# One over rms by exp and ln on ScalarE in place of a power on GpSimd, and a fourth buffer of float64 words

## Chip, cores and metric

One core of a Trainium2 chip runs the whole kernel. The metric is the device time of one execution in microseconds (us). Several executions agree within some 0.3%.

## The reference, cut to what matters

Attention with normalised queries and keys, and behind it two stages of dense layers, all in float32:

```python
q_n = q / sqrt(mean(q * q) + 1e-6) * g_q          # k_n alike with g_k; over the 64 of a head
scores = q_n @ k_n.T / 8
attn = exp(scores - max) / (sum + 1e-9)
x = attn @ v                                       # 4 batches, 12 heads, 448 rows, 64 columns
h = x @ w_in;  x = maximum(0.01 * h, h) @ w_out    # 768 -> 2048 -> 768, 1792 rows
y = ((x @ w1) * (x @ w2)) @ w3 @ w_last            # 768 -> 1024 -> 1024 -> 768
```

The weights come as float64. Each product is made of three matmuls: every operand is split into a high and a low part (`wh`, `wl`; `xh`, `xl`), and high x high, high x low and low x high are added up.

## The kernel before, in words

TensorE (PE) does all products and transposes, ScalarE (ACT) exp, copies and the rounding to the high parts, VectorE (DVE) the low parts, sums and reductions, GpSimd (POOL) the normalisation of the softmax and some subtractions. SyncE's queue (SP) issues most loads; ACT's queue issues loads of weights, POOL's the stores of converted weights.

**Attention** goes by pairs of heads, 24 of them, t from 0 to 23. `load_rows` (L127) loads the rows of q and k of a pair three pairs ahead. `statistics` (L137), also three pairs ahead, squares them on ACT (L149), sums on DVE (L150), makes mean plus epsilon `ss` (L151) and takes it to the power of -0.5 on POOL (L153), with a tile `power` full of -0.5; L154 scales the part of q. `keys` (L192) multiplies the rows of k (L200), transposes them on PE into `pk` (L205), and writes the high and low keys `kh` on ACT (L214) and `kl` on DVE (L215), two buffers each. The transposes are told to come behind the last scores of the pair before. `scores` (L221) makes the scores, DVE moves them from PSUM into tiles `p` (L250), nine buffers, ACT applies exp in place (L259), DVE makes the reciprocal of the sums (L264, L265), POOL normalises (L268). `p_transpose` (L275) transposes p on PE (L282), DVE and ACT copy the result (L104, L102). `values` multiplies with v.

**Weights.** The class `Weights` converts float64 words to float32 by integer arithmetic: a load of a tile's words (`load`, L386; the DMA is L398) into `w64`, three buffers; `to_float32` (L400) with one instruction on POOL (L416), two on ACT (L418, L421) and two on DVE (L423, L427); `split` (L430) with the rounding on ACT (L452) and the low part on DVE (L180), and where a tile is needed again stores of it from POOL's queue (L444, L455). The first three loads are issued by SP's queue once the queries of the second pair are on their way; each later one by ACT's queue, behind the rounding of the tile that was split last (`self.rounded`). `work` (L459) sets the order: split tile t, load tile t+3, convert tile t+1.

**Order.** The attention's steps and the dense layers' matmuls are interleaved by `fill`, which spends an estimated time of matmuls per step; the conversions are pulled by the matmuls (`pump`) two tiles ahead. A scheduler with a timing model then sets each engine's order from these steps, their priorities and `issue_after`. The first pairs come alone; the product of the two last weight matrices begins with the fifth pair. Batches 0 and 1 go through the dense layers beside the attention, two groups of weights for batch 0 alone; these are stored and loaded again for batch 1. From some 820 us only the last two batches' dense layers are left.

Of the kernel before, what the change touches and what calls it, by code (L numbers as in the profile page):

```python
# [8 lines left out]
F32 = mybir.dt.float32  # L9
F32R = mybir.dt.float32r  # L10
U32 = mybir.dt.uint32
AF = mybir.ActivationFunctionType
ALU = mybir.AluOpType
# [4 lines left out]
B, H, S, D = 4, 12, 448, 64  # L18
NT = B * S
DM, FF, F2 = 768, 2048, 1024  # L20
P = 128
CP = 112
NCH = S // CP
# [11 lines left out]
CONVERT_PRIORITY = 100  # L35
STATS_AHEAD = 3
KEYS_AHEAD = 1
P_TILES = 9
TOGETHER = 2000
COMBINE_SLOTS = 5, 17  # L40
EARLY = 2
# [6 lines left out]
def attention_then_moe(  # L48
# [22 lines left out]
    nc = tc.nc  # L71
# [4 lines left out]
    def right(**kw):  # L76
        return heads_only.enter_context(tc.tile_pool(side="right", **kw))

    const = ctx.enter_context(tc.tile_pool(name="const", bufs=1))
# [2 lines left out]
    io = right(name="io", bufs=2)  # L82
    att = right(name="att", bufs=2)
    small = right(name="small", bufs=4)
    cv = right(name="cv", bufs=3)
    dram = ctx.enter_context(tc.tile_pool(name="dram", bufs=1, space=DRAM))
    psum = ctx.enter_context(tc.tile_pool(name="psum", bufs=8, space=PSUM))

    def bank(name):
        return psum.tile([P, 512], F32, tag="ps", name=name)  # L90
# [2 lines left out]
    ident = const.tile([P, P], F32, name="ident")  # L93
    gg = const.tile([P, 2], F32, name="gg")
    gqk = const.tile([P, 1], F32, name="gqk")
    power = const.tile([CP, 2, 2, NCH], F32, name="power")
    wc = dram.tile([NO, P, K2, P], F32, name="wc")
    xd = dram.tile([B - PB, KD, P, S], F32, name="xd")

# [12 lines left out]
    start = {}  # L112
# [14 lines left out]
    def load_rows(t):  # L127

        if t >= NH // 2:
            return  # L130
        b, j = divmod(2 * t, H)
        x = pairs[t]["rows"] = io.tile([CP, 2, 2, NCH, D], F32, tag="qk", name="qk_sb", bufs=2)
        for part in (1, 0):
            src = qk[b, j : j + 2, :, part].rearrange("h p c d -> p h c d")
            start["dma"] = nc.sync.dma_start(x[:, part], src)

    def statistics(t):  # L137

        if t >= NH // 2:
            return  # L140
        x = pairs[t]["rows"]
        ss = small.tile([CP, 2, 2, NCH], F32, tag="ss", name="ss", bufs=2)
        after = exps.get(t - STATS_AHEAD)
        for part in (1, 0):
            y = x[:, part]
            if part:
                y = io.tile([CP, 2, NCH, D], F32, tag="sq", name="sq", bufs=1)
            with tc.issue_after(after.ins) if after else ExitStack():
                nc.scalar.activation(y, x[:, part], AF.Square)  # L149
            nc.vector.tensor_reduce(ss[:, part], y, axis=AX.X, op=ALU.add)  # L150
        nc.vector.tensor_scalar(ss, ss, 1.0 / D, 1e-6, op0=ALU.mult, op1=ALU.add)  # L151
        rs = small.tile([CP, 2, 2, NCH], F32, tag="rs", name="rs", bufs=4)
        nc.gpsimd.tensor_tensor(rs, ss, power, op=ALU.pow)  # L153
        nc.vector.tensor_scalar_mul(rs[:, 0], rs[:, 0], -1.0 / D**0.5)  # L154
        pairs[t]["scale"], pairs[t]["rk"] = rs[:, 0], rs[:, 1]

    def load(t):

        if t >= NH // 2:
            return  # L160
        b, j = divmod(2 * t, H)
        pairs[t]["qt"] = io.tile([P, S], F32, tag="qt", name="qt_sb")
        dma = nc.sync.dma_start(pairs[t]["qt"], qt[b, j : j + 2].rearrange("h d s -> (h d) s"))
        start["dma"] = dma
        if t == 1:
            start["ins"] = dma
# [15 lines left out]
    def prep(t):  # L182

        if t >= NH // 2:
            return
        x = pairs[t]
        x["qh"] = att.tile([P, S], F32R, tag="qh", name="qh", bufs=2)
        copy("A", x["qh"], x["qt"])
        x["ql"] = att.tile([P, S], F32R, tag="ql", name="ql", bufs=2)
        subtract("P", x["ql"], x["qt"], x["qh"])  # L190

    def keys(t):  # L192

        if t >= NH // 2:
            return
        x = pairs[t].pop("rows")
        kn = x[:, 0].rearrange("p h c d -> p (h c d)")
        kn = kn.rearrange("p (c h d) -> p c h d", c=NCH, h=2)
        rk = pairs[t]["rk"].unsqueeze(3).to_broadcast([CP, 2, NCH, D])
        nc.vector.tensor_tensor(kn.rearrange("p c h d -> p h c d"), x[:, 1], rk, op=ALU.mult)  # L200
        pk = bank("pk")
        scored = pairs[t - 1].get("scored") if t else None
        with tc.issue_after(scored.ins) if scored else ExitStack():
            for c in range(NCH):
                nc.tensor.transpose(  # L205
                    pk[:, c * CP : (c + 1) * CP],
                    kn[:, c].rearrange("p h d -> p (h d)"),
                    ident[:CP, :CP],
                )
        x = [att.tile([P, S], F32R, tag=part, name=part, bufs=2) for part in ("kh", "kl")]  # L210
        pairs[t]["kh"], pairs[t]["kl"] = x
        kh, kl = (y.rearrange("q (p c) -> q p c", c=NCH) for y in x)
        pk = pk[:, :S].rearrange("q (c p) -> q p c", c=NCH)
        one = nc.scalar.activation(kh, pk, AF.Copy, scale=gqk)  # L214
        nc.vector.scalar_tensor_tensor(  # L215
            kl, pk, gqk, kh.bitcast(F32), op0=ALU.mult, op1=ALU.subtract
        )
        if t == 0:
            start["keys"] = one

    def scores(t, half):  # L221
# [24 lines left out]
        for c in chunks:  # L246
            for e, h in enumerate(pair):
                p = h["p"][c] = att.tile([CP, S], F32, tag="p", name="p", bufs=P_TILES)
                low = small.tile([CP, 1], F32, tag="low", name="low", bufs=8)
# [88 lines left out]
    def attention_steps():  # L338

        for t in range(NH // 2 + 2):  # L340
            ranked(values, t - 2)
            yield 2 * t
            for half in range(2):
                s = 2 * t + half
                for kc in range(NCH):
                    ranked(p_transpose, s - 2, kc)
                    yield s
                ranked(scores, t, half)
                for _ in range(NCH):
                    yield s  # L350
                if half:
                    ranked(keys, t + KEYS_AHEAD)
                    ranked(load, t + 2)
                    ranked(statistics, t + STATS_AHEAD)
                else:
                    load_v(2 * t)
                    ranked(prep, t + 1)
                    load_rows(t + STATS_AHEAD)
                run_later()
                yield s  # L360


    class Weights:
# [22 lines left out]
        def load(self, t):  # L386
            src, wide = self.sources[t][:2]
            n = self.size(t)
            if isinstance(src, tuple):
                return  # L390
            if not wide:
                self.raw[t] = wp.tile([P, WT], F32, tag="raw", name="raw")
                nc.sync.dma_start(self.raw[t][:, :n], src)
                return
            x = self.words[t] = cv.tile([P, WT, 2], U32, tag="w64", name="w64")
            eng = nc.sync if t < 3 else nc.scalar
            with tc.issue_after((start["ins"] if t < 3 else self.rounded).ins):
                eng.dma_start(x[:, :n], src.rearrange("p (n t) -> p n t", t=2))  # L398

        def to_float32(self, t):  # L400
# [57 lines left out]

        def work(self):  # L459
            n = len(self.sources)  # L460
            for t in range(-3, n):
                if t >= 0:
                    self.split(t)
                    yield
                for u, wide in ((t + 2, False), (t + 3, True)):
                    if 0 <= u < n and self.sources[u][1] == wide:
                        self.load(u)
                        yield
                if 0 <= t + 1 < n and self.sources[t + 1][1]:
                    yield from self.to_float32(t + 1)  # L470
# [479 lines left out]


    with tc.high_priority():
        nc.vector.memset(power, -0.5)
        make_identity(nc, ident)
        load_rows(0)
        statistics(0)
        load(0)
        nc.sync.dma_start(gg, g)
        nc.vector.tensor_tensor(gqk, gg[:, 0:1], gg[:, 1:2], op=ALU.mult)
        prep(0)  # L960
        keys(0)
    for t in range(1, STATS_AHEAD):
        load_rows(t)
        if t == 1:
            load(1)
        statistics(t)
        if t < KEYS_AHEAD:
            keys(t)
# [32 lines left out]
    with tc.tile_pool(name="comb", bufs=1) as pool:  # L1001
# [17 lines left out]
        n = slots[1] - slots[0]  # L1019
        fill(combine_weights(ws, pool, hi, lo), comb_ns, n * per_slot, slots[1], slots[0] * per_slot)  # L1020
    pool = first_pair.enter_context(tc.tile_pool(name="mlp", bufs=1))
    n = PB * H + 2
# [50 lines left out]
```

## Time and profile before

| what | value |
|---|---|
| median of 3 runs | 1240.68 us (1239.51 to 1243.39) |
| the profiled execution's own time | 1246.91 us |
| its span, first to last instruction | 1245.1 us |
| mean granted TensorE clock | 0.965 |
| busy: PE, DVE, ACT, POOL | 1162.3, 777.3, 656.6, 465.5 us |

The span is the time between the first and the last instruction of the profiled execution; the execution's own time has a little more around it. Engines work in order, each through its own queue, and wait for each other by semaphores; a wait is put down to the engine or transfer that ended it. Busy time of PE includes time at a lower clock, and PEld is PE's loading of weights, beside the matmuls.

### The profile page before, as it was taken

What the parts mean: (1) busy time and instruction counts of PE and PEld (TensorE: products, weight loads), DVE (VectorE), ACT (ScalarE), POOL (GpSimd) and SP (SyncE); (2) the same over time, 40 slices, a digit from 0 to 9 for tenths busy, and PEclk for the clock granted to TensorE, in tenths of its full rate; (3) what the DMA queues carried; (4) which work ended last, traced back from release to release, by engine and by line L of the source; (5) the groups of instructions that cost most, each with busy time, mean ns of one, the idle gap of its engine ahead of it and who ended that gap; (6) DMA issues with size and microseconds to landing.
All of it is one profiled execution on the core that took longest, in us unless ns stands there. A gap on an engine that the chain in (4) does not pass through costs nothing.

```text
span 1245.1 us, 16895 instructions
## 1 busy us (share of the span) xinstructions
PE 1162.3 (93%) x6096; PEld 969.6 (78%) x6096; DVE 777.3 (62%) x1440; ACT 656.6 (53%) x1295; POOL 465.5 (37%) x498
## 2 busy tenths in 40 slices
PE   2589999899879999999899999999999999899998
PEld 1357778666658888788788888888999999699997
DVE  6897677778753375758865565277436365964553
ACT  6766576677644465566564564345443434533431
POOL 5876666778853456357744434200000000000000
PEclk8669999999889999999999999999999999999999
DMA  7423336768576543543442342062202121211212
GB/s 231 147 96 106 117 117 208 270 209 293 182 283 203 161 152 122 181 139 124 164 128 69 109 176 84 33 201 80 81 28 77 34 77 51 64 39 64 71 36 98
DMA packets 65380, 158.92 MB, mean 128 GB/s; under 512 B 7440, under 2 KB 32784, under 8 KB 65296
## 3 DMA queue, kind: packets, MB, share of 16 engines
q1 hardware_dynamic: 45504, 73.16, 18.6%
q10 hardware_dynamic: 11088, 50.07, 12.3%
q0 software_dynamic: 8704, 34.61, 6.9%
q8 instruction: 48, 0.79, 0.2%
q14 instruction: 36, 0.29, 0.1%
HBM read 114.95 MB, written 42.86 MB: 127 GB/s over the span
## 4 chain that ended last, share of the span: by engine, by line
PE 70%; DVE 13%; DMA 8%; POOL 3%; ACT 3%; issue 2%; SPq 0%; ACTq 0%; POOLq 0%; DVEq 0%
PE ps_mm L495 24%; PE ps_o L495 13%; PE ps_b L495 9%; PE ps_c L495 5%; PE po L124 4%; PE ps L124 4%; PE pt L282 4%; PE pw L495 4%; DMA w<-w_in 3%; DMA w<-w_out 2%; DVE raw L423 2%; PE ps_a L495 2%; DVE p L250 2%; POOL p L268 2%; DVE wl L180 1%
## 5 line engine op out<-in xcount | busy, mean ns | idle before, releaser
L268 POOL TENSOR_SCALAR p<-p,r 112x448 f32<-112x448 f32 x192 | 152.4, 809 | 62.0 <-DVE r L265 37.9
L180 DVE TENSOR_TENSOR wl<-raw,wh 128x512 fp32r<-128x512 f32 (+1 forms) x136 | 122.0, 898 | 81.6 <-ACT wh L452 41.5
L259 ACT ACTIVATE p<-p,low 112x448 f32<-112x448 f32 x192 | 126.6, 661 | 50.4 <-DVE p L250 50.3
L495 PE MATMUL ps_mm<-xh,wh 128*128 128x448 f32 x384 | 142.8, 372 | 7.6 <-DMA wh<-kept_first_mlp_h 3.0
L495 PE MATMUL ps_mm<-xl,wh 128*128 128x448 f32 x384 | 147.3, 384 | 0.8 <-POOL xl L180 0.8
L495 PE MATMUL ps_mm<-xh,wl 128*128 128x448 f32 x384 | 142.6, 371 | 0.0
L250 DVE TENSOR_SCALAR_CACHE_REDUCE p<-ps,rs 112x448 f32<-112x448 f32 x192 | 122.0, 677 | 30.1 <-PE ps L124 30.1
L282 PE MATMUL pt<-ident,p 112*112 112x112 f32 x768 | 106.5, 278 | 32.7 <-POOL p L268 29.7
L282 PEld LDWEIGHTS pt<-ident,p 112*112 112x112 f32 x768 | 87.7, 143 | 56.9 <-POOL p L268 35.2
L418 ACT ACTIVATE w<-w 128x768 uint32<-128x768 uint32 (+1 forms) x80 | 63.9, 798 | 93.5 <-DMA w<-w_in 32.7
L495 PE MATMUL ps_mm<-gh,wh 128*128 128x448 f32 x288 | 107.1, 374 | 5.7 <-ACT wh L452 5.1
L423 DVE SCALAR_TENSOR_TENSOR raw<-w,raw 128x768 uint32<-128x768 uint32 (+1 forms) x80 | 79.1, 989 | 50.4 <-ACT w L421 49.9
L495 PE MATMUL ps_mm<-gl,wh 128*128 128x448 f32 x288 | 109.8, 381 | 0.0
L495 PE MATMUL ps_mm<-gh,wl 128*128 128x448 f32 x288 | 106.3, 369 | 0.6 <-DMA wl<-kept_first_mlp_l 0.6
L495 PE MATMUL ps_o<-gl,wh 128*128 128x448 f32 x288 | 104.8, 368 | 0.0
L495 PE MATMUL ps_o<-gh,wl 128*128 128x448 f32 x288 | 101.3, 368 | 0.0
L495 PE MATMUL ps_o<-gh,wh 128*128 128x448 f32 x288 | 100.0, 368 | 0.0
L416 POOL TENSOR_SCALAR raw<-w 128x768 f32<-128x768 f32 (+1 forms) x80 | 72.3, 906 | 65.0 <-DMA w<-w_in 16.4
L153 POOL TENSOR_TENSOR rs<-ss,power 112x16 f32<-112x16 f32 x24 | 72.3, 3011 | 46.6 <-DVE ss L151 46.2
L495 PEld LDWEIGHTS ps_mm<-xh,wh 128*128 128x128 f32 x384 | 73.0, 190 | 15.9 <-issue 4.2
L495 PEld LDWEIGHTS ps_mm<-xl,wh 128*128 128x128 f32 x384 | 73.3, 191 | 12.8 <-issue 6.2
L124 PE MATMUL po<-pth,v_sb 112*64 112x448 f32 x384 | 79.6, 557 | 1.6 <-ACT pth L102 1.6
(133 smaller groups left out, 2698.7 us busy)
## 6 DMA issues: line engine op xcount, KB each, us to landing
w<-w_in ACTq DMA_DIRECT2D x16, 768.0 KB, 5.2
w<-w_out ACTq DMA_DIRECT2D x24, 512.0 KB, 3.8
w<-w ACTq DMA_DIRECT2D x16, 768.0 KB, 4.5
qk_sb<-qk SPq DMA_DIRECT2D x48, 224.0 KB, 3.8
w<-w3t ACTq DMA_DIRECT2D x16, 512.0 KB, 3.8
kept_first_mlp<-raw POOLq DMA_DIRECT2D x16, 384.0 KB, 4.3
kept_first_mlp<-raw POOLq DMA_DIRECT2D x24, 256.0 KB, 2.9
kept_second_mlp<-raw POOLq DMA_DIRECT2D x16, 384.0 KB, 2.8
```

What stands on the lines that cost most here:

```text
L124: one = nc.tensor.matmul(out, a, x, start=begin, stop=end)
L153: nc.gpsimd.tensor_tensor(rs, ss, power, op=ALU.pow)
L180: e.tensor_tensor(out, x, y.bitcast(F32), op=ALU.subtract)
L250: nc.vector.tensor_scalar(p, ps[c % 2][e], x["scale"][:, e, c : c + 1], None, op0=ALU.mult, op1=ALU.min, accum_out=low,)
L259: exps[t] = nc.scalar.activation(p, p, AF.Exp, bias=low, scale=-1.0, accum_out=x["sums"][:, e, c : c + 1])
L268: nc.gpsimd.tensor_scalar(h["p"][c], h["p"][c], r[:, e, c % 2 : c % 2 + 1], 1.0, op0=ALU.mult, op1=ALU.mult)
L282: nc.tensor.transpose(pt[:, c * CP : (c + 1) * CP], h["p"][c][:, kc * CP : (kc + 1) * CP], ident[:CP, :CP],)
L416: nc.gpsimd.tensor_scalar(out, h, 0.0, 1.0, op0=ALU.mult, op1=ALU.mult)
L418: nc.scalar.activation(low, low, AF.Copy, scale=2.0**-29)
L423: nc.vector.scalar_tensor_tensor(top, high, 3, top, op0=ALU.logical_shift_left, op1=ALU.bitwise_or)
L495: nc.tensor.matmul(ps[:, :n], a, x, start=begin, stop=end, skip_group_check=on)
```

## The change

One over rms is now exp(-0.5 ln(ss)) on ACT, with a Newton step of three instructions on DVE. A table that holds Exp and Ln is named at the start. There are four buffers of words, loads go four tiles ahead, and the first four are issued by SP's queue. Eight p tiles stand in place of nine, and one buffer each of `kh` and `kl` in place of two.

```diff
-P_TILES = 9
+P_TILES = 8
...
-    cv = right(name="cv", bufs=3)
+    cv = right(name="cv", bufs=4)
...
-    power = const.tile([CP, 2, 2, NCH], F32, name="power")
...
         rs = small.tile([CP, 2, 2, NCH], F32, tag="rs", name="rs", bufs=4)
-        nc.gpsimd.tensor_tensor(rs, ss, power, op=ALU.pow)
+        y = small.tile([CP, 2, 2, NCH], F32, tag="y", name="y", bufs=2)
+        nc.scalar.activation(y, ss, AF.Ln)
+        nc.scalar.activation(rs, y, AF.Exp, scale=-0.5)
+        nc.vector.scalar_tensor_tensor(y, rs, -0.5, rs, op0=ALU.mult, op1=ALU.mult)
+        nc.vector.tensor_tensor(y, y, ss, op=ALU.mult)
+        nc.vector.scalar_tensor_tensor(rs, y, 1.5, rs, op0=ALU.add, op1=ALU.mult)
         nc.vector.tensor_scalar_mul(rs[:, 0], rs[:, 0], -1.0 / D**0.5)
...
-        x = [att.tile([P, S], F32R, tag=part, name=part, bufs=2) for part in ("kh", "kl")]
+        x = [att.tile([P, S], F32R, tag=part, name=part, bufs=1) for part in ("kh", "kl")]
...
-            eng = nc.sync if t < 3 else nc.scalar
-            with tc.issue_after((start["ins"] if t < 3 else self.rounded).ins):
+            eng = nc.sync if t < 4 else nc.scalar
+            with tc.issue_after((start["ins"] if t < 4 else self.rounded).ins):
                 eng.dma_start(x[:, :n], src.rearrange("p (n t) -> p n t", t=2))
...
-            for t in range(-3, n):
+            for t in range(-4, n):
...
-                for u, wide in ((t + 2, False), (t + 3, True)):
+                for u, wide in ((t + 2, False), (t + 4, True)):
...
     with tc.high_priority():
-        nc.vector.memset(power, -0.5)
+        nc.scalar.preload_act_table_set("natural_log_exp_and_others")
         make_identity(nc, ident)
```

## Rows read from the trace of the kernel before

**Rows 1.** The page's busy times: us, share of the span, instructions.

```profile
PE 1162.3 (93%) x6096; PEld 969.6 (78%) x6096; DVE 777.3 (62%) x1440; ACT 656.6 (53%) x1295; POOL 465.5 (37%) x498
```

**Rows 2.** Busy us (count) by stage: PE, PEld, DVE, ACT, POOL; clock, DMA share, GB/s.

```profile
0.00:100.00 100.00, 56.08 (x265) 37.64 (x267) 83.45 (x166) 67.28 (x135) 71.01 (x60) 0.73 0.47 148
...
200.00:330.00 130.00, 117.53 (x644) 87.81 (x643) 103.95 (x183) 90.36 (x188) 99.06 (x120) 0.97 0.72 251
...
590.00:620.00 30.00, 25.15 (x129) 21.09 (x128) 26.53 (x38) 17.69 (x32) 20.90 (x18) 0.94 0.50 182
```

**Rows 3.** Waits of PE, 0 to 110 us: total us, times, longest.

```profile
PE pt L282 <- POOL p L268: 29.7, 8, 17.4
```

**Rows 4.** The chain of waits, 0 to 110 us: start, length, what.

```profile
10.53 3.36 POOL rs L153
...
16.24 0.69 DVE p L250 x2
...
30.61 2.91 POOL rs L153
...
34.71 7.15 POOL p L268 x6
...
70.48 2.88 POOL rs L153
```

**Rows 5.** Waits of PE, 190 to 400 us.

```profile
PE ps L124 <- ACT y L582: 3.3, 1, 3.3
PE ps L124 <- DVE xl L180: 3.1, 1, 3.1
...
PE po L124 <- ACT pth L102: 1.6, 1, 1.6
```

**Rows 6.** Timeline of ACT and its queue from 194 us: start, length, what, idle time before.

```profile
194.21 0.33 ACTq L398 DMA_DIRECT2D w<-w_in  x1
...
199.37 0.93 ACT L418 ACTIVATE w<-w 128x768 uint32<-128x768 uint32 x1 [2.35 <-DMA w<-w_in]
199.38 0.33 ACTq L398 DMA_DIRECT2D w<-w_in  x1
...
206.56 0.33 ACTq L398 DMA_DIRECT2D w<-w_in  x1
```

**Rows 7.** Waits of ACT, 190 to 330 us.

```profile
ACT w L418 <- DMA w<-w_out: 17.1, 7, 4.5
...
ACT w L418 <- DMA w<-w_in: 8.8, 7, 2.4
```

**Rows 8.** Groups by form: count, busy us, mean ns, idle us before them.

```profile
L268 POOL TENSOR_SCALAR p<-p,r 112x448 f32<-112x448 f32 x192 | 152.4, 809 | 62.0 <-DVE r L265 37.9 <-PE ps_mm L495 16.3 <-PE pt L282 3.6
...
L153 POOL TENSOR_TENSOR rs<-ss,power 112x16 f32<-112x16 f32 x24 | 72.3, 3011 | 46.6 <-DVE ss L151 46.2 <-DVE rs L154 0.2
...
L452 ACT ACTIVATE wh<-raw 128x768 fp32r<-128x768 f32 x32 | 26.8, 838 | 13.7 <-PE ps_mm L495 11.1 <-DMA wl<-kept_first_mlp_l 2.3
...
L149 ACT ACTIVATE sq<-qk_sb 112x512 f32<-112x512 f32 x24 | 15.0, 626 | 20.3 <-DMA qk_sb<-qk 20.3
...
L151 DVE TENSOR_SCALAR ss<-ss 112x16 f32<-112x16 f32 x24 | 8.9, 370 | 0.2
...
L265 DVE RECIPROCAL r<-r 112x4 f32<-112x4 f32 x48 | 8.3, 174 | 0.9
```

**Rows 9.** POOL's busy time (count) on L153 by stage; clock, DMA share, GB/s.

```profile
0.00:100.00 100.00, 17.92 (x6) 0.73 0.47 148
...
200.00:330.00 130.00, 10.98 (x4) 0.97 0.72 251
```

**Rows 10.** Waits over the whole span: total us, times, longest.

```profile
DVE raw L423 <- ACT w L421: 49.9, 38, 4.9
...
POOL rs L153 <- DVE ss L151: 46.2, 9, 12.4
```

**Rows 11.** The load of ACT's table, of the groups.

```profile
L149 ACT ACT_TABLE_LOAD x1 | 1.3, 1283 | 0.7 <-PEq L1063 0.7
```

## The prediction

> **What bounds the kernel now.** I began with the page. TensorE (PE) is busy 93% of the span, 1162.3 us of 1245.1 [rows 1]; its work isn't touched by the change, so the change can only be worth what it takes from the 82.8 us in which PE stands idle, and from the time in which PE runs at its lower clock. The table of busy times by stage says where these are [rows 2]. From 0 to 100 us PE is busy 56.1 of 100 us, at a mean granted clock of 0.73: part of that work ran at the lower of the two levels (1.2 and not 2.4 GHz), after PE had stood idle. From 200 to 330 us it lacks 12.5 of 130 us, at 0.97. From 590 to 620 it lacks 4.9 us. That is 61.3 us of the 82.8; the rest lies scattered, where PE is all but full and an earlier input is worth little. In these three stages VectorE (DVE) is the fullest of the engines that feed PE: 83.5 of 100, 104.0 of 130, 26.5 of 30 us [rows 2].
>
> Then I asked who releases PE. Up to 110 us it waits 29.7 us for normalised p tiles from GpSimd (POOL), 17.4 us of it in one piece [rows 3]. The chain of waits of that stretch runs through the power operation of L153 three times, for 3.36, 2.91 and 2.88 us [rows 4]. Two of them deliver a value that the next step on DVE needs (first p at 16.24 us). The middle one only stands in POOL's queue, ahead of the normalisation that starts at 34.71. From 190 to 400 us the larger waits of PE are for ScalarE's (ACT) y, 3.3 us, DVE's xl, 3.1 us, and ACT's pth, 1.6 us [rows 5].
>
> Why is ACT late there? Its timeline shows a load of float64 words issued at 194.21 us, and ACT taking those very words at 199.37, after 2.35 us of waiting; the next load goes out at 199.38 [rows 6]. Three buffers are there, but a load is issued only behind the rounding of the tile three before it, and the conversion has by then run ahead to the last words. From 190 to 330 us ACT stands 17.1 + 8.8 = 25.9 us in such waits [rows 7], and exp, the copies of p and the rounding stand behind it in its queue.
>
> **The change, part by part.**
>
> *The power operation goes.* 24 of them took 3.011 us each, 72.3 us of POOL [rows 8]; six lie in the stage to 100 us and four in that from 200 to 330 [rows 9]. In their place come Ln and Exp over 16 elements a row on ACT, and three instructions on DVE. No row has an activation so short. From 626 ns for 512 elements (L149) and 838 ns for 768 (L452) [rows 8] the slope is 0.83 ns an element, which makes 215 ns for 16: an estimate, 0.43 us for the two. A DVE instruction of the same shape, 112x16, is L151, mean 370 ns [rows 8]; three make 1.11 us, and at the 174 ns of the reciprocal of L265, also a tiny one, 0.52 us [rows 8]. I take 1.11, the row of the same shape. So the value arrives after 0.43 + 1.11 = 1.54 us in place of 3.0. On the chain up to 110 us that gives 3.36 + 2.91 + 2.88 = 9.15 us less two values at 1.54, a gain of 6.1 us. The other four of the six pairs in this stage put 1.11 us each on a DVE that is 83% full: 4 x 1.11 x 0.83 = 3.7 us lost, though the least is 4 x 0.52 x 0.83 = 1.7. Stage 0 to 100: **-2.4 us**, between -8 (nothing of the small work shows, and the clock gains from less idle time) and +4 (the chain passes over to DVE and only the added work stays).
>
> L151 has more than twice L265's mean, though it does little more; POOL's normalisation has a mean of 809 ns [rows 8]. The Trainium skill (SBUF — State Buffer, SBUF: two separate sides) says that a DVE instruction with two SBUF inputs and a GpSimd instruction that reads SBUF take one port pair exclusively, and that the loser blocks for the whole of the other. All three new DVE instructions have two SBUF inputs, so this rule speaks against the change: with one whole normalisation waited for in each trio it would be 0.52 + 0.81 = 1.33 us, 0.22 more a pair, and over ten pairs the sum below would stand some 2 us higher.
>
> *The fourth buffer.* Each load now follows the rounding of the tile four before it, at the same place of ACT's queue but one tile further ahead, so it has one more round of about 5 to 7 us (194.21 to 199.38 to 206.56, [rows 6]) to land. ACT's 25.9 us of waiting should mostly go, unless the transfers themselves fill the DMA engines, whose share from 200 to 330 us is 0.72 [rows 2]. What PE can get back there is 12.5 us of idle time and 3% of clock, 3.9 us: 16.4. ACT is the releaser in 3.3 + 1.6 of the 8.0 us named above [rows 5]; I take that share, 0.61, as what comes back: -10.0 us. Next late is DVE. Against it stand four pairs' small instructions, 4 x 1.11 x 0.80 = 3.6 us. Stage 200 to 330: **-6.4 us**, between -16.4 and +4.
> At the start the fourth load goes to SP's queue, behind the first two transfers of q, and so stands ahead of the rows of later pairs and of their q; each issue takes some 0.33 us [rows 6] and 768 KB. I cost it at nothing, because the heads ahead are loaded three pairs early; if that cover is gone, one load's time of 5 us falls on the second pair.
> From 590 to 620 I expect nothing: DVE has 3.5 of 30 us to spare there.
>
> *One buffer of keys.* The new kh and kl are written after the transposes into pk, which the kernel queues on PE behind the last scores of the pair before. PE works in order, so the readers of the old keys are done by then: nothing. If an extra wait came, it would stand on ACT, in front of exp.
>
> *Eight p tiles.* A pair fills eight. The ninth lets one p of the next pair be written before a first tile of this pair is given back by the transposes of its first head; but these stand ahead of the next pair's scores in the program, so that p has its tile by the time its scores are there: nothing. Where the scheduler puts scores first, DVE waits for one normalisation and its transposes, 0.81 us [rows 8] in a few pairs, inside the bounds above.
>
> **Sum.** -2.4 - 6.4 = -8.8 us. The profiled execution took 1246.91 us, 1.8 more than its span; it would take 1238.1. It lies 6.2 us above the median of the runs shown, 1240.68, so the forecast by that median is **1231.9 us**.
>
> **Rivals.**
> 1. *New waits take the place of the old* (slower). POOL waited 46.2 us for ss in 9 of 24 cases, up to 12.4 [rows 10]; ACT now stands in that wait at Ln, with exp of p behind it, and DVE then waits for Exp, with the next p and the words' conversion behind it. DVE waits for ACT today at L423 38 times for 49.9 us, 1.3 us each [rows 10]. Ten pairs lie in the stages where DVE is full: 10 x (1.3 + 1.11) = 24 us, against 6.1 and at most 10.0 gained: +8, 1248.7 us. It decides where DVE's idle time, 16.5 us to 100 and 26 us from 200 to 330, is used up. Against it: ss and Ln are three pairs ahead, so most of the order leaves slack. Chance 0.18.
> 2. *DVE bounds the stage from 200 us*, and the earlier words only wait for it. Then -2.4 + 3.6 = +1.2 stays: 1241.9 us. For it speak 104.0 busy us of 130, against it ACT's waits. Chance 0.17.
> 3. *The loads were the whole matter*: all 16.4 us come back, the start gives 8, and 590 to 620 gives 2: -26.4, 1214.3 us. For it speaks that a single wait of ACT explains most of what is late, against it DVE's share of these stages. Chance 0.14.
> 4. *Tables are switched.* Today ACT loads one table, 1283 ns, before everything [rows 11]. If Ln and Exp lay in different ones, each pair would load two; 20 loads in the ten pairs are 25.7 us on ACT: -8.8 + 25.7 = +16.9, 1257.6 us. The change names one set up front, so I give it 0.04. The Trainium skill (ScalarE: Activation LUTs, Table sets: the hidden batching unit) has both functions in the set that the change names, which by that rule leaves one load; no run here shows it yet.
>
> **How the numbers follow.** The forecast has 0.47; its own range is 1224 to 1237. A measurement of this kernel tells about 0.3% from no change, 3.7 us. Faster: 0.47 + 0.14 = 0.61; within: 0.17; slower: 0.18 + 0.04 = 0.22. The range of 8 in 10 reaches to rival 3 below and to rival 1 above, 1212 to 1249, and leaves out the table case and half of rival 1's tail.
>
> **What would show it.** Right: no L153 on POOL; one table load; ACT's waits for w from 190 to 330 us fall from 25.9 to under 8; first p before 16.24 us; PE busy from 0 to 100 above 56.1 us, and from 200 to 330 at a higher share than 0.90. Wrong: DVE waiting for Exp or ACT for ss by more than 1 us a time; the waits for w still there, with a DMA share near 0.9; PE's idle time in these stages as before while POOL's busy time fell by 72 us.

## The result, and the profile after

The changed kernel took 1232.58 us (median of 5 runs, 1229.40 to 1235.36), the kernel before 1243.04 us (5 runs) beside it: a ratio of 0.9917, with a 95% interval of 0.9888 to 0.9947. It is faster by some 10 us; forecast were 8.8. Run again in the study it came to 0.9913 [0.9888, 0.9937]. The profiled execution has a span of 1227.6 us, against 1245.1.

The page's busy times after, to be held against [rows 1]:

```profile
PE 1157.6 (94%) x6096; PEld 966.4 (79%) x6096; DVE 777.9 (63%) x1511; ACT 662.7 (54%) x1343; POOL 390.2 (32%) x474
```

POOL lost 75 us, 72.3 of them the power. DVE has 71 instructions more and the same busy time. PE's idle time went from 82.8 to 70.0 us, and PE's own busy time fell by 4.7. These two traces lie further apart than the medians, 17.5 us against 10.5: the profiled execution of the kernel before, 1246.91 us, was longer than all five of its runs above, and the one after, 1229.40, the shortest of its five. So a second trace of the changed kernel is read beside it, that of **e0_whole**: its span is 1235.9 us, and PE is idle there for 76.8 us.

The stages of [rows 2] after, and 330 to 400 us, which the prediction did not look at (columns as there):

```profile
0.00:100.00 100.00, 60.34 (x279) 37.62 (x280) 83.82 (x187) 71.41 (x155) 51.69 (x56) 0.74 0.49 155
...
200.00:330.00 130.00, 122.42 (x675) 93.92 (x672) 108.15 (x205) 92.72 (x200) 91.00 (x123) 0.95 0.72 252
330.00:400.00 70.00, 63.02 (x339) 50.61 (x337) 32.19 (x73) 33.26 (x71) 23.58 (x34) 0.93 0.68 240
590.00:620.00 30.00, 29.63 (x161) 23.65 (x158) 24.94 (x48) 19.97 (x41) 21.88 (x23) 1.00 0.42 140
```

The same stretch of the kernel before:

```profile
330.00:400.00 70.00, 62.41 (x319) 49.41 (x318) 34.74 (x73) 32.32 (x68) 36.64 (x43) 0.90 0.62 218
```

PE is busier in the three stages that the prediction named; from 590 to 620 us it is all but full, where the prediction gave nothing. In e0_whole the last two of them are alike (120.61 and 29.43 us busy), but from 0 to 100 us PE is busy 56.27 us, as it was before the change.

The waits of PE after, 0 to 110 us, which answer to [rows 3]:

```profile
PE pt L286 <- POOL p L272: 20.7, 8, 10.4
PE pk L209 <- DVE y L155: 12.9, 1, 12.9
```

The wait for POOL's normalised p is 9.0 us shorter, as one expects with the power no longer ahead of it. The wait for the first pair's keys, in the second line, is 1.6 us longer than the 11.3 us of the kernel before. All waits of PE in this stretch come to 43.9 us before, 39.5 here and 43.6 in e0_whole, so that the changed kernel's start is not clearly shorter. The waits of ACT for words, 190 to 330 us, against the 17.1 + 8.8 us of [rows 7]:

```profile
ACT w L422 <- DMA w<-w_out: 8.9, 4, 3.1
ACT w L422 <- DMA w<-w_in: 5.0, 6, 1.4
```

They fell from 25.9 to 13.9 us, about half. The new instructions, in the groups by form (busy us, mean ns | idle us before):

```profile
L155 DVE SCALAR_TENSOR_TENSOR y<-rs 112x16 f32<-112x16 f32 x24 | 7.8, 326 | 3.6 <-ACT rs L154 3.6
...
L156 DVE TENSOR_TENSOR y<-y,ss 112x16 f32<-112x16 f32 x24 | 7.0, 290 | 0.4
...
L157 DVE SCALAR_TENSOR_TENSOR rs<-y,rs 112x16 f32<-112x16 f32 x24 | 5.2, 217 | 0.5
L154 ACT ACTIVATE rs<-y 112x16 f32<-112x16 f32 x24 | 5.1, 212 | 0.4
L153 ACT ACTIVATE y<-ss 112x16 f32<-112x16 f32 x24 | 5.1, 212 | 8.6 <-DVE ss L150 8.4
L957 ACT ACT_TABLE_LOAD x1 | 1.3, 1283 | 0.7 <-PEq L1067 0.7
```

Ln and Exp take 0.42 us together, the Newton step 0.33 + 0.29 + 0.22 = 0.83 us, and one table is loaded.

**A clock for the stages.** Work moves into and out of a stage with fixed ends, so the experiments are also read by the time at which the n-th matmul of the expert layers beside the attention (into `ps_mm`, 2016 in all) ended, counted in each trace. This clock has noise of its own: after and e0_whole are one kernel, and stand 3.2 us apart at the 384th product and 6.3 at the 2000th.

| kernel (us) | 1st | 192nd | 384th | 768th | 2000th |
|---|---|---|---|---|---|
| before | 219.8 | 306.4 | 388.6 | 496.1 | 839.1 |
| f4_kh1 | 219.9 | 306.8 | 385.7 | 493.1 | 835.9 |
| f2_power_moved | 219.7 | 304.5 | 382.6 | 492.1 | 835.2 |
| e2_exp | 216.9 | 307.8 | 381.6 | 489.1 | 829.0 |
| f1_exp_pad | 214.7 | 305.8 | 381.9 | 489.3 | 828.2 |
| f3_p8 | 220.7 | 311.6 | 392.5 | 499.9 | 841.6 |
| e3_room | 222.8 | 313.8 | 395.0 | 502.8 | 844.8 |
| e1_loads | 217.2 | 300.1 | 390.0 | 497.6 | 839.5 |
| after | 219.5 | 303.6 | 379.9 | 487.7 | 825.4 |
| e0_whole | 220.7 | 304.4 | 383.1 | 491.5 | 831.7 |
| g1_late_after | 217.1 | 299.6 | 369.3 | 484.1 | 823.9 |
| g2_late_exp | 215.8 | 305.1 | 371.1 | 480.9 | 818.2 |
| e4_no_table_named | 230.9 | 316.7 | 395.9 | 503.6 | 844.0 |
| e5_no_newton | 215.5 | 297.0 | 370.6 | 479.8 | 821.4 |

### The profile page after: what moved, and what is told of

Its sections match the earlier page's. It is cut to its first block, busy times and chain, and to the rows that moved or that the text cites. A ratio compares the mean times of both kernels' runs of the same rounds, so it can differ in the third digit from the quotient of the medians.

```text
span 1227.6 us, 17006 instructions
## 1 busy us (share of the span) xinstructions
PE 1157.6 (94%) x6096; PEld 966.4 (79%) x6096; DVE 777.9 (63%) x1511; ACT 662.7 (54%) x1343; POOL 390.2 (32%) x474
## 4 chain that ended last, share of the span: by engine, by line
PE 64%; DVE 7%; DMA 4%; ACT 1%; issue 1%; POOL 1%; SPq 0%; ACTq 0%; DVEq 0%; POOLq 0%
PE ps_mm L499 26%; PE ps_o L499 13%; PE ps_b L499 9%; PE ps_c L499 5%; PE po L123 3%; PE pt L286 3%; PE ps L123 3%; PE ps_a L499 2%; DVE ol L184 1%; DVE wl L184 1%; DMA wh<-kept_first_mlp_h 1%; DMA qk_sb<-qk 1%; DMA x_f<-xd 1%; DMA w<-w_out 1%; DVE acc L863 1%
## 5 line engine op out<-in xcount | busy, mean ns | idle before, releaser
L184 DVE TENSOR_TENSOR wl<-raw,wh 128x512 fp32r<-128x512 f32 (+1 forms) x136 | 113.9, 839 | 74.9 <-ACT wh L705 35.1
L286 PE MATMUL pt<-ident,p 112*112 112x112 f32 x768 | 107.2, 278 | 25.7 <-POOL p L272 20.7
L427 DVE SCALAR_TENSOR_TENSOR raw<-w,raw 128x768 uint32<-128x768 uint32 (+1 forms) x80 | 76.0, 949 | 51.1 <-ACT w L425 50.9
L425 ACT ACTIVATE w<-w 128x768 f32<-128x768 f32 (+1 forms) x80 | 63.1, 789 | 45.6 <-POOL raw L420 45.6
L499 PEld LDWEIGHTS ps_mm<-xl,wh 128*128 128x128 f32 x384 | 73.2, 191 | 10.8 <-issue 4.9
```

The costliest lines, as they stand in the source:

```text
L184: e.tensor_tensor(out, x, y.bitcast(F32), op=ALU.subtract)
L286: nc.tensor.transpose(pt[:, c * CP : (c + 1) * CP], h["p"][c][:, kc * CP : (kc + 1) * CP], ident[:CP, :CP],)
L425: nc.scalar.activation(h, h, AF.Copy, scale=2.0**-112)
L427: nc.vector.scalar_tensor_tensor(top, high, 3, top, op0=ALU.logical_shift_left, op1=ALU.bitwise_or)
L499: nc.tensor.matmul(ps[:, :n], a, x, start=begin, stop=end, skip_group_check=on)
```

## The experiments

All were timed in five rounds against the kernel before on the same chip; a ratio stands with its 95% interval.

### The parts, one by one

**e1_loads**: the changed kernel with the power back on POOL, so the fourth buffer and what makes room for it.

```diff
-        y = small.tile([CP, 2, 2, NCH], F32, tag="y", name="y", bufs=2)
-        nc.scalar.activation(y, ss, AF.Ln)
...
-        nc.vector.scalar_tensor_tensor(rs, y, 1.5, rs, op0=ALU.add, op1=ALU.mult)
+        nc.gpsimd.tensor_tensor(rs, ss, power, op=ALU.pow)
```

> The changed kernel with the power operation put back on POOL: only the fourth buffer, the loads four ahead, eight p tiles and one buffer of keys are left. Theory A (the forecast: the loads bring most of it, 10.0 us without the small instructions' 3.6): ratio 0.992, some 1233 us against 1243; ACT's waits for w from 190 to 330 us near the 13.9 of the changed kernel. Theory B (the power's leaving POOL brings all): ratio 1.000. Theory C (a new order of the schedule, whatever the edit): anywhere within 5 us of either kernel, and the parts don't add up.

Measured: 1.0034 [1.0014, 1.0055]. Buffer and room together win nothing; they lose 4 us.

**e2_exp**: the kernel before with Ln, Exp and the Newton step alone: three buffers, nine p tiles, two of keys.

```diff
-        nc.gpsimd.tensor_tensor(rs, ss, power, op=ALU.pow)
+        y = small.tile([CP, 2, 2, NCH], F32, tag="y", name="y", bufs=2)
+        nc.scalar.activation(y, ss, AF.Ln)
...
+        nc.vector.scalar_tensor_tensor(rs, y, 1.5, rs, op0=ALU.add, op1=ALU.mult)
```

> The kernel before with only 1 / rms by Ln, Exp and the Newton step: three buffers, loads three ahead, nine p tiles, two buffers of keys. Theory A: -2.4 us to 100 us and +3.6 after 200, so +1, ratio 1.001. Theory B: the whole gain, ratio 0.992. Theory C: within 5 us, and not the whole less the first run's part. The first transposes of p should begin near 31 us as in the changed kernel if the start's gain is the power's.

Measured: 0.9921 [0.9894, 0.9948]. This part alone brings what the whole change brings.

**e3_room**: the kernel before with eight p tiles and one buffer of keys, but three of words.

```diff
-P_TILES = 9
+P_TILES = 8
...
-tag=part, name=part, bufs=2) for part in ("kh", "kl")]
+tag=part, name=part, bufs=1) for part in ("kh", "kl")]
```

> The kernel before with eight p tiles and one buffer of keys alone. Theories A and B: ratio 1.000, as nothing waits for either. Theory C: off by up to 5 us through another order. If the tiles were needed: slower by up to 10 us, with waits of DVE at the p instruction for PE's transposes.

Measured: 1.0068 [1.0044, 1.0091], a loss of 8.5 us by the steps that the prediction cost at nothing. Against it e1_loads, 1.0034, says that the fourth buffer is worth 4.2 us, give or take some 4 (the half widths of the two intervals, 0.0021 and 0.0024, put together as the root of the sum of their squares).

**e0_whole**: the changed kernel again, beside these three.

> The changed kernel again, on the chip of these runs, to have all four against the same runs of before: ratio 0.992 within 0.003 by every theory. By theory A it is the product of the first two ratios, by theory C it isn't.

Measured: 0.9913 [0.9888, 0.9937]. The parts give -9.8 + 4.2 = -5.6 us, the whole -10.8. The difference, 5.2 us, is as large as the half widths of the three intervals put together, 5.2 us, so whether the parts add up is not settled.

### What makes the room dear

**f3_p8** has only the eight p tiles:

```diff
-P_TILES = 9
+P_TILES = 8
```

**f4_kh1** has only the one buffer of keys:

```diff
-tag=part, name=part, bufs=2) for part in ("kh", "kl")]
+tag=part, name=part, bufs=1) for part in ("kh", "kl")]
```

> The kernel before with eight p tiles alone. If the ninth tile carries the 8.5 us that eight tiles and one buffer of keys cost together: 1.0068, with the loss before 100 us and from 220 to 310 us as there. If it is the keys: 1.000. If it is only another order of the schedule: neither this nor the next gives it, or both do in part.

> The kernel before with one buffer of kh and kl alone. If the keys carry the loss: 1.0068, with ACT or DVE waiting at kh or kl for PE's scores. If the p tiles do: 1.000. With the run before it the two should give 1.0068 as a product if the costs are of waits, and need not if of the order.

Measured: f3_p8 1.0067 [1.0042, 1.0092], f4_kh1 0.9998 [0.9978, 1.0018]. The whole loss is the ninth p tile; the keys cost nothing, and f4_kh1 has the order of the kernel before on every engine. With nine tiles the scheduler puts four transposes of p in between two scores of the third pair; with eight it does so only from the fourth pair on, and from the third pair on the orders of PE, DVE, ACT and POOL differ. Waits of PE in f3_p8, 200 to 400 us:

```profile
PE ps_mm L495 <- ACT wh L452: 10.3, 4, 4.3
PE ps_mm L495 <- DMA wl<-kept_first_mlp_l: 6.2, 1, 6.2
```

In the kernel before these are 7.9 us for `wh` and 3.0 for kept words, so two waits in the dense layers grew by 5.6 us together, while that for `y` fell from 3.3 to 0.7 us. None of these is a wait for a p tile, and in f3_p8 DVE's waits at p are all for scores, 28.9 us against 30.1 before. By the table the time is lost between the first and the 192nd product, 90.9 us against 86.6. That the missing tile acts by way of the order is what the rows suggest; the order was not held fixed against the number of tiles.

### Addresses or work?

e2_exp also frees the 64 bytes of `power` among the constants, and so moves the addresses of what lies behind it. **f1_exp_pad** is e2_exp with a tile of that size kept there:

```diff
+    power = const.tile([CP, 2, 2, NCH], F32, name="power")
...
+        nc.vector.memset(power, -0.5)
```

**f2_power_moved** is the kernel before with its `power` moved to another pool:

```diff
-    power = const.tile([CP, 2, 2, NCH], F32, name="power")
...
+    pw_pool = right(name="pw_pool", bufs=1)
+    power = pw_pool.tile([CP, 2, 2, NCH], F32, name="power")
```

> The kernel with Ln, Exp and the Newton step alone, and a tile of 64 bytes a row, filled once and never read, at the place where the tile of powers stood, so that all later tiles of that side have the addresses of the kernel before. Theory L (the addresses set the step of the matmuls of the last layers): the ps_o matmuls of the last phase start 206 to 207 ns apart as in the kernel before, not 203, the last phase takes 399 and not 396 us, and the ratio is 0.9945, 3 us above the 0.9921 without the tile. Theory M (ACT's other table, or less heat, makes the step): 203 ns and 0.992 stay.

> The kernel before, with only the tile of powers moved from the constants to a pool of the other side; the power stays on POOL. Theory L: ps_o step 203 ns, last phase 396 us, ratio 0.9975 (3 us). Theory M: 207 ns, ratio 1.000. Were the addresses the whole of what Ln and Exp alone gave: 0.992.

Measured: f1_exp_pad 0.9917 [0.9896, 0.9938], f2_power_moved 0.9988 [0.9968, 1.0007]. The gain stays where the addresses are the old ones and does not come with the new ones: it is not the addresses. What is left is the work itself and the order that the scheduler makes of it: f1_exp_pad has the order of e2_exp, f2_power_moved that of the kernel before, and these two orders differ on all four engines from the first pairs on. No run held the order fixed against the work. The addresses do show in one group of matmuls, before and in f2_power_moved:

```profile
L495 PE MATMUL ps_o<-gl,wh 128*128 128x448 f32 x288 | 104.8, 368 | 0.0
```

```profile
L496 PE MATMUL ps_o<-gl,wh 128*128 128x448 f32 x288 | 104.1, 365 | 0.0
```

The mean goes from 368 to 365 ns with nothing but the place of a tile; more on this at the end.

### Where the fourth buffer's gain goes

By the table, e1_loads is 12.6 us ahead of the mean of f3_p8 and e3_room at the 192nd product (300.1 against 312.7), and 3.8 at the 384th (390.0 against 393.8). So it does win time up to 306 us, and loses 8.8 of it by 390. The timeline of e1_loads, DMA issues on the queues of ACT and SP from 344 us (start, length, what):

```profile
344.68 2.24 ACTq L398 DMA_DIRECT2D w<-w_in  x4
...
350.07 0.35 SPq L439 DMA_DIRECT2D wh<-kept_first_mlp_h  x1
353.11 0.34 SPq L439 DMA_DIRECT2D wl<-kept_first_mlp_l  x1
356.29 0.32 SPq L439 DMA_DIRECT2D wh<-kept_first_mlp_h  x1
359.79 0.32 SPq L439 DMA_DIRECT2D wl<-kept_first_mlp_l  x1
```

Four loads of 768 KB are issued together. Their `issue_after` names the last rounding, and as the tiles in between are kept ones, which are read back and not rounded, all four follow one rounding. They landed at 350.0, 353.0, 356.2 and 359.7 us, and SP's reads of the kept words go out one by one just then. That is no chance: by the trace SP's queue waits, before each of these four reads, for one of the loads to land; the read reports its own landing by the very semaphore that this load had (101 to 104 in the trace). The waits of SP's queue in e1_loads, 344 to 361 us:

```profile
SPq L439 <- DMA w<-w_in: 10.5, 4, 3.1
```

The first read then took until 361.8 us. PE waits for those reads, while the next rounding of words comes only at 436.5 us. The waits of PE in e1_loads, 300 to 400 us:

```profile
PE ps_mm L495 <- DMA wh<-kept_first_mlp_h: 8.6, 1, 8.6
PE ps L124 <- ACT y L582: 5.7, 1, 5.7
```

The kernel before has the same row with 3.0 us and three loads together. To test it, **g1_late_after** (from the changed kernel) and **g2_late_exp** (from e2_exp, three buffers) put these loads on SP's queue, behind reads of kept words (the diff is g1_late_after's; g2_late_exp has 3 where it has 4):

```diff
-                    nc.sync.dma_start(y, part)
+                    self.kept = nc.sync.dma_start(y, part)
...
-            eng = nc.sync if t < 4 else nc.scalar
-            with tc.issue_after((start["ins"] if t < 4 else self.rounded).ins):
+            late = t >= 4 and isinstance(self.sources[t - 4][0], tuple); eng = nc.sync if t < 4 or late else nc.scalar
+            with tc.issue_after((start["ins"] if t < 4 else self.kept if late else self.rounded).ins):
```

> The changed kernel, with the four w_in loads that are issued together at 345 us put on SP's queue, each behind a read of the second half's kept words, so that they no longer land in front of the first half's. Theory (the loads' gain is given back where these loads meet the kept reads): TensorE's wait for the kept words, 6.1 us, falls under 3.1 us, and the ratio goes from 0.9915 to between 0.986 and 0.9895. Rival 1 (the wait is only one face of a stretch that is full anyway): the wait falls, the ratio stays within 0.002 of 0.9915. Rival 2 (SP's queue, now with four more issues of 0.33 us and their waits for a free buffer, holds the next pairs' q and v): 0.994 or more, and TensorE waits longer after 380 us.

> The kernel before with only the Ln, Exp and Newton part (three buffers of words, nine p tiles, two of keys), and the three w_in loads moved to SP's queue in the same way. Theory: its wait for the kept words, 4.9 us, falls to the 3 us or less of the kernel before, and 0.9921 becomes 0.988 to 0.9905: the best of all versions. Rival 1 (the stretch is full anyway): within 0.002 of 0.9921. Rival 2 (SP's queue is held): 0.995 or more.

Measured: g1_late_after 0.9892 [0.9867, 0.9917], g2_late_exp 0.9862 [0.9835, 0.9890]. In g2_late_exp the loads went out from 411.9 to 415.3 us. Its waits of PE, 300 to 400 us, and its stage from 330 us:

```profile
PE ps_mm L499 <- DMA wh<-kept_first_mlp_h: 0.2, 1, 0.2
```

```profile
330.00:400.00 70.00, 69.83 (x395) 57.66 (x394) 28.28 (x77) 33.16 (x77) 24.83 (x34) 1.00 0.62 196
```

and the same of e2_exp, whose code differs only in these loads:

```profile
PE ps_mm L499 <- DMA wh<-kept_first_mlp_h: 4.9, 1, 4.9
```

```profile
330.00:400.00 70.00, 65.09 (x356) 53.23 (x355) 33.15 (x75) 32.67 (x70) 26.97 (x35) 0.95 0.66 227
```

The wait of 4.9 us is gone and the granted clock is 1.00 in place of 0.95: PE, idle for those 4.9 us, had run part of the stage at the lower of its levels. The lead is 10.5 us at the 384th product, 2.7 of which were there at the 192nd, before these loads are issued; 8.2 are left at the 768th. More came than the theory had (0.988 to 0.9905), which priced the wait without the clock. For the kernel with three buffers the gain from moving the loads is shown: the intervals of e2_exp and g2_late_exp do not meet.

By which way the loads held the reads up is less sure. In e2_exp SP's queue does not wait for them. There the first read went out at 343.5 us and landed at 353.1, 9.6 us later, with the DMA engines full; in g2_late_exp it took 4.2 us, with a DMA share of 0.74 in the same stretch. The stretch in e2_exp:

```profile
340.00:355.00 15.00, 10.09 (x52) 7.37 (x49) 10.01 (x17) 8.07 (x14) 7.66 (x9) 0.85 1.02 391
```

With the loads, the conversion of their words moved too, from 341 to 418 us and later. The runs do not separate its part from that of the transfers.

For the changed kernel it is likely but not settled, since the intervals of g1_late_after and e0_whole overlap. Waits of PE in the changed kernel, 300 to 400 us:

```profile
PE ps_mm L499 <- DMA wh<-kept_first_mlp_h: 7.0, 2, 6.1
```

In e0_whole the same matmul waits 6.2 us; its row names DVE, but the read landed 0.1 us before that matmul began. In g1_late_after no wait for kept words is longer than 0.5 us there, and the 384th product comes 10.6 us earlier than in the trace after (4.0 of them at the 192nd already), but of these 3.6 are left at the 768th. TensorE does wait longer after 380 us, as the expectation's second rival said, but for kept words and not for q or v. Stage and waits of PE in g1_late_after after 370 us:

```profile
370.00:435.00 65.00, 59.10 (x316) 47.30 (x314) 27.16 (x56) 30.09 (x58) 20.01 (x25) 0.95 0.73 234
```

```profile
PE ps_mm L499 <- DMA wh<-kept_first_mlp_h: 3.3, 2, 2.9
PE ps_mm L499 <- DMA wl<-kept_first_mlp_l: 2.6, 1, 2.6
```

One of the four loads went out at 402.6 us, ahead of the last six of the second half's reads, and the other three among and behind them, from 412.2 us on; PE now waits 5.9 us for kept words. g2_late_exp, with three loads, all among and behind the last reads, waits 2.2 us there.

g2_late_exp is the fastest version here, 1228.89 us against 1244.68 beside it: Ln and Exp, three buffers, nine p tiles, and the loads out of the way of the kept words.

### The table and the Newton step

**e4_no_table_named** is the changed kernel without the line that names a set.

```diff
-        nc.scalar.preload_act_table_set("natural_log_exp_and_others")
```

> The changed kernel without the line that names one set of functions up front: the program then holds 49 table loads in place of one, two for each of the 24 pairs. At the 1.28 us of the one load that is 61.6 us more of ScalarE. Theory of the prediction's rival 4 (each load of the ten pairs in the stages short of input is on the path): 25.7 us over the changed kernel, 1.012 of the kernel before. Rival 1 (all 48 show): 1.041. Rival 2 (ScalarE, busy 54% of the span, takes most of them in its waits): 8 us or less, 0.998 or below.

Measured: 1.0024 [1.0006, 1.0043], so (1.0024 - 0.9913) x 1240 = 13.8 us over e0_whole. Its groups on ACT:

```profile
L153 ACT ACT_TABLE_LOAD x24 | 30.8, 1283 | 0.4
L154 ACT ACT_TABLE_LOAD x23 | 29.5, 1283 | 0.4
L148 ACT ACT_TABLE_LOAD x1 | 1.3, 1283 | 0.7 <-PEq L1066 0.7
```

A forty-ninth is in front of an exp of p. Of the 61.6 us of added loads under a quarter shows in the time; that lies between the prediction's price for its rival 4, 25.7 us, and the 8 us of the case in which ACT takes them in its waits. By its trace 10 to 11 us are lost before the first product of the expert layers (230.9 us against 219.5 and 220.7), where ACT's busy time from 0 to 100 us rose from 71.41 to 83.01.

**e5_no_newton** leaves the Newton step out of the computation.

```diff
-        nc.vector.scalar_tensor_tensor(y, rs, -0.5, rs, op0=ALU.mult, op1=ALU.mult)
-        nc.vector.tensor_tensor(y, y, ss, op=ALU.mult)
-        nc.vector.scalar_tensor_tensor(rs, y, 1.5, rs, op0=ALU.add, op1=ALU.mult)
```

> The changed kernel without the three Newton instructions on VectorE (the Newton step of 1 / rms is left out of the computation). They take 24 x 0.83 = 20 us of VectorE, 0.83 us a pair. Theory of the prediction (in the ten pairs of the stages in which VectorE is 80% full they stand on the path, 0.8 x 0.83 x 10 = 6.7 us): 0.986 instead of 0.9915. Rival (the value is wanted late enough, VectorE has room for it): within 0.002 of 0.9915. A third case, the order of the program shifts and the ratio rises above 0.994, would say that the time hangs on the order more than on the cost of these instructions.

Measured: 0.9902 [0.9871, 0.9933]. It can't be told from the changed kernel, 0.9913: the difference is 0.0011, with some 0.004 either way if the half widths of the two intervals are put together (the root of 0.0031 and 0.0025 squared). That is 1.4 us for the step, at most some 6. The 6.7 us that the prediction's way of counting gives lie just outside; that the step is free is not shown either. Without the three instructions the order differs on all four engines too, so this run weighs the step and a new order together.

## Why the prediction was right, and where it was not

The number was right, 1231.9 forecast and 1232.6 measured, and so was the case, faster. But three of its steps were off, in sizes that cancel: +1.2, -10.0 and nothing were forecast for the three parts, and -9.8, -4.2 and +8.3 us measured. That the sum came within 2 us of the measured change is luck, and more so that the time came within 0.7 us: the kernel before, measured beside the changed one, took 2.4 us more than the median from which the forecast starts.

**Ln and Exp: priced at -2.4 + 3.6 = +1.2 us, worth -9.8.** By the table, the mean of e2_exp and f1_exp_pad against that of the three kernels with the power and nine p tiles: at the first product 215.8 against 219.8, so -4.0 us (forecast -2.4); up to the 192nd 306.8 against 305.9, so +4.9 in that stretch (forecast +3.6). Both of these steps hold roughly, though in the changed kernel itself the first is not seen (219.5 and 220.7 at the first product). What failed is the step after them: the prediction stopped at 330 us, and for 590 to 620 us said "I expect nothing". Up to the 384th product the lead grows by 4.8 us (381.8 against 385.6, where the three kernels with the power spread over 6.0), and by the 2000th by another 4.2 (828.6 against 836.7). PE's busy time says the same with less spread: from 330 to 400 us it is 60.9 to 62.4 us in those three and 65.1 and 64.9 in e2_exp and f1_exp_pad, and from 590 to 620 us 25.2 to 25.3 against 28.5 and 29.4. In the first of these stretches the largest wait of PE in the kernel before, 300 to 400 us, is gone in e2_exp and in f1_exp_pad:

```profile
PE ps_mm L495 <- ACT wh L452: 4.6, 1, 4.6
PE ps L124 <- ACT y L582: 3.3, 1, 3.3
PE ps_mm L495 <- DMA wh<-kept_first_mlp_h: 3.0, 1, 3.0
```

The power went from all 24 pairs, and the sum priced ten. What set that wait on ACT, the power's time on POOL or the other order of the engines, was not isolated.

**The fourth buffer: priced at -10.0 in the stage from 200 us, worth some 4 us in all, give or take 4.** Up to the 192nd product the price is about right: e1_loads gains 8.1 us there on the two kernels with the same room (82.9 us between the first and the 192nd against 91.0), and the changed kernel some 7 on e2_exp and f1_exp_pad. "Next late is DVE" is what failed: next late are the kept words, which PE waits for at 346 to 362 us, and there the gain is given back. A load that goes out earlier was followed only to its own reader. What it runs into was asked for the start alone.

**Eight p tiles: priced at nothing, cost 8.3 us.** The argument "that p has its tile by the time its scores are there" followed the order of the program and not that of the scheduler, which changes with the ninth tile. The prediction's other case, DVE waiting for a p tile, did not come in f3_p8. One buffer of keys at nothing was right, within the 0.002 that f4_kh1 can tell.

**The sign posts.** Right: no power on POOL, one table load, PE's share from 200 to 330 us 0.94 against 0.90. Right in one trace only: PE's busy time from 0 to 100 us, 60.34 us against 56.1, but 56.27 in e0_whole. Wrong: ACT's waits for words fell to 13.9 us, not under 8, and the first p came later, not before 16.24 us. The timeline of DVE after, from 10 us, says why:

```profile
9.99 0.58 DVE L963 TENSOR_TENSOR gqk<-gg 128x1 f32<-128x1 f32 x1 [0.71 <-DMA gg<-g]
10.49 0.16 DVE L155 SCALAR_TENSOR_TENSOR y<-rs 112x16 f32<-112x16 f32 x1
10.57 1.10 DVE L150 TENSOR_SCALAR ss<-ss 112x16 f32<-112x16 f32 x1
11.59 0.16 DVE L156 TENSOR_TENSOR y<-y,ss 112x16 f32<-112x16 f32 x1
...
17.18 0.67 DVE L254 TENSOR_SCALAR_CACHE_REDUCE p<-ps,rs 112x448 f32<-112x448 f32 x1
```

The first pair's Newton step stands in DVE's queue behind the gains' product, which waits for its load, and behind the second pair's `ss`; the power had stood in POOL's queue, free of both, and the first pair's had ended at 9.24 us, while DVE still waited for the gains. What Ln and Exp win at the start, 4.0 us in the kernels with nine p tiles, fits the other place that the prediction named, POOL's queue ahead of the normalisation.

**The rivals.** New waits (1): DVE waited for Exp 3.6 us in all and at most 0.9 us at a time, ACT for `ss` 8.4 us in 8 waits, of which the longest, 3.0 us, is over the 1 us that was named as a sign of being wrong; the price of 24 us for it was far off. DVE as the bound (2) would have left +1.2 us, and 10 were won. Loads as the whole matter (3): they brought the least. Tables (4): one load with the named set, 49 without, so its condition is shown to be real and its price, 25.7 us, to be about twice the cost. The Trainium skill (ScalarE: Activation LUTs, Table sets: the hidden batching unit) has both functions in the set that is named, and the trace's one load agrees.

**The Newton step's price** was 1.11 us a pair; it measured 0.83. Undisturbed, each of its instructions takes 0.17 us, as in the rows above; in the trace after, 53 of the 72 have no computing instruction of POOL beside them, and they average 0.17. The other 19 average 0.51, 0.65 and 0.71 us by line, but 7 of them take no more than 0.18. One of the lengthened ones, DVE and POOL from 49 us:

```profile
49.23 1.14 POOL L184 TENSOR_TENSOR ql<-qt_sb,qh 128x448 fp32r<-128x448 f32 x1 [1.99 <-ACT qh L101]
...
49.25 1.15 DVE L156 TENSOR_TENSOR y<-y,ss 112x16 f32<-112x16 f32 x1
```

Here a step that otherwise takes 0.17 us lasts as long as POOL's instruction beside it. The Trainium skill (SBUF — State Buffer, SBUF: two separate sides) says that such a pair excludes each other for a whole instruction; this row agrees, and 12 of the 72 steps were lengthened, where the prediction's estimate of 1.33 us a trio had one in each, 24.

## What to carry to other kernels

A step that is removed from an engine's queue in every round of a loop is worth looking up in every round, and not only in the stages where the bounding engine is idlest; most of this change's gain came elsewhere. For a load that is issued earlier, follow what it will share the queues with: here four loads whose words were rounded some 90 us later held up four reads that TensorE stood waiting for, and moving the three of the smaller version gave 0.6%. And a change of several parts is to be taken apart even where its forecast came true: one part here brought the whole gain, one gave by its trace two thirds of its own back, and one cost 8.3 us.

## What the runs showed of the hardware

The place of a 64-byte tile among the constants changes the pace of some matmuls: with `power` there (before, e1_loads, e3_room, f1_exp_pad, f3_p8, f4_kh1) two matmuls into `ps_o` start 207 ns apart, where it is gone or moved (after, e0_whole, e2_exp, f2_power_moved) 203 ns. Other groups go the other way (one form into `ps_b` 202 to 207 ns, one into `ps_mm` 204 to 206), and the sum is within what f2_power_moved can tell from no change. Why the place matters stays open.
